# Gated linear attention and a squared-ReLU MLP on one core: an instruction order worked out again with other durations and rank shifts

## The chip, the core and the metric

The kernel runs on one core of one Trainium2 chip. The metric is the device time of one execution in microseconds (us). Three executions of the kernel before took 702.45, 704.4 and 1441.48 us; the median is 704.4 us. A profile was taken of one execution.

## The reference, cut to what matters

```python
# q, k, v, a_re, a_im: (4, 8, 768, 48), fp32
mag = sqrt(a_re**2 + a_im**2)
a = (a_re + 1j * a_im) * minimum(mag, 0.999) / (mag + 1e-6)
for t in range(768):                       # per batch and head, state S is 48 x 48, complex
    S = a[t][:, None] * S + outer(k[t], v[t])
    y[t] = q[t] @ S.real
x = y.transpose(0, 2, 1, 3).reshape(3072, 384)
h = x @ w_in                               # 384 x 2048
out = maximum(h, 0)**2 @ w_out             # 2048 x 384
```

## The kernel before

The 3072 rows are cut into six tiles of 512 time steps (`NU = 6`, index `n` below). For each tile there are three stages.

* **chain(n)**, mostly VectorE (DVE) and ScalarE (ACT). The gates are loaded in natural layout, normalised (`roots`, `normalise`, lines 956 to 999), multiplied up over groups of four steps (`inner`, lines 1011 to 1019), transposed on TensorE (PE) in `totals` (line 1065), scanned on DVE (`scan`, `product`, lines 1157 to 1224) and transposed back (`back`). Then `inverse`, `factors` and `twist` make the inverse products (1033 to 1045, 1114 to 1129), and `apply` multiplies q and k by the running products (1285 to 1299). `gather` moves k to another layout by DMA (line 1340).
* **pairs(n)**, for four pairs of heads. `turn_pe` (tiles 0 and 1, PE transposes of line 1401, ACT copies of line 1405) or `turn` (later tiles: DVE transposes of line 1378 and DMAs) lays q and k out by feature. `score` multiplies them (PE line 1419) and masks the result (DVE line 1422); `keep` makes the state sums (PE line 1447, DVE lines 1456 and 1458); `mix` makes y (PE lines 1471 and 1475, ACT copy of line 1481), and SyncE (SP) DMAs bring y into `xT`.
* **dense(n, grp)**, two groups of 256 rows: `part_of` is x times w_in (PE line 1511), `relu` the activation (ACT lines 1542 and 1543). The second product is plain for tile 0 (PE line 1557) and otherwise `seven` or `eight`, a scheme with fewer products (PE line 1619, DVE lines 1634 and 1643).

The weights arrive as 64-bit numbers and are made into fp32 on the chip: `fetch` loads a piece (GpSimd queue, POOL, line 817), `convert` makes it fp32 (ACT lines 830 and 834, DVE lines 836, 840 and 843). Eight pieces are w_in and eight are w_out. `inspect` reads them once more near the end, and `verdict` decides whether the fast result holds.

No engine chooses its order at run time. Every stage only hands **steps** to a planner (`Plan.add`): an engine, a duration, what it reads and writes, and a rank. `Plan.order` plays these steps through once while the kernel is being built. At each moment it takes, among the steps of an engine whose inputs are ready by its own clock, the one of the lowest rank. The start times that it arrives at give the order in which the instructions are emitted, and so the fixed order of every engine's queue and of every DMA queue. The durations are thus never a limit on the chip: they only decide the order.

Ranks are pairs such as `(PAIR, n)`, and 100 times the first plus the second is compared: pairs of tile n have 100 + n, its chain 200 + n, dense work 300 + n, the conversion of w_in 200.3 and that of w_out 200.6. `Plan.shift` adds to these numbers by hand, for a group of steps (`groups`) or for one step (`single`), numbered in the order in which they were added.

Two further things hang on the planner. Where PE is planned to stand idle and one of the banks d0 to d2 is free, `order` puts **idle products** there (a product of the identity with itself, emitted from line 735), which write nothing that is used; their number is the planned idle time, less 0.3 us, over `EACH`. And a PE step that follows a planned stop of over 2.5 us is planned as slower for a while (`STOP`, `COLD`):

```python
if spare and stop > self.FILL:
    self.fill[n] = int((stop - 0.3) / self.EACH), spare[0]
elif stop > self.STOP:
    warm = t + self.COLD
```

Of the kernel before, what the change touches and what calls it, by code (L numbers as in the profile page):

```python
# [480 lines left out]
class Plan:  # L481
# [7 lines left out]
    FILL, EACH = 0.8, 0.22  # L489
# [8 lines left out]
    def add(self, eng, dur, reads, writes, fn, rank, wire=None, group=None, after=(), slack=False):  # L498

        n = len(self.steps)  # L500
# [4 lines left out]
        for k in reads:  # L505
            deps.update(self.wrote.get(k, (None, ()))[1])
        for k in writes:
# [12 lines left out]
        self.steps.append((eng, dur, sorted(deps), fn, rank, wire, slack))  # L520
# [10 lines left out]
    def order(self):  # L531
# [11 lines left out]
        bus, warm = 0.0, 6.0  # L543
# [18 lines left out]
        for _ in steps:  # L562
# [10 lines left out]
            _, dur, _, _, _, wire, _ = steps[n]  # L573
# [48 lines left out]
def fast_path(ctx, tc, q, k, v, a_re, a_im, moe_w_in, moe_w_out, out, flag):  # L622
# [6 lines left out]
    C = 128  # L629
# [129 lines left out]
    def dma(q, reads, writes, fn, rank, size, lat=1.8, group=None):  # L759
        name, dur = ("POOL", 0.55) if q is pool else ("SP" if q is sp else "ACT", 0.6)  # L760
        step(name, dur, reads, writes, fn, rank, (lat, size), group)
# [52 lines left out]
    def fetch(i, early=True):  # L814
# [3 lines left out]
            (CONV, i), 2 * PW * 4 * C, 4.0)  # L818

    def convert(i):  # L820
# [11 lines left out]
        if mixed:  # L832

            step("ACT", 1.92, keys + [("lo", i)], [("lo", i, 1)], lambda: act.activation(
                out=part(F16, 1), in_=part(I16, 3), func=AF.Copy, scale=2.0 ** -60), rank)
        step("DVE", ts2(PW), keys, wk, lambda: dve.tensor_scalar(
# [9 lines left out]
    def inspect(i):  # L846
# [6 lines left out]
        if i == 0:  # L853
# [5 lines left out]
            rank, 2 * PW * 4 * C)  # L859
# [61 lines left out]
    def chain(n):  # L921
# [81 lines left out]
        def inner(z):  # L1003
# [16 lines left out]
            for c in range(1, W):  # L1020
                step("DVE", 2 * tt(m) + 0.06, [("a", z)], key(z, 0), lambda c=c: terms(c), ahead)
                step("DVE", 2 * tt(m // 2) + 0.06, key(z, 0), [("a", z)],
                     lambda c=c: joined(c), ahead)
            xh = xn.rearrange("p r (h d) -> p r h d", h=H)[:, :, ts(z, HH)]
            step("ACT", ac(Z // W), [("a", z)], [("xn", 0, z), ("xn", 1, z)],
# [33 lines left out]
        def turned(src, put, by, keys, rk):  # L1059
# [6 lines left out]
            step("PE", 0.12 * NM, keys, [(b,)], go, rk)  # L1066
# [8 lines left out]
        def totals(j):  # L1075
# [4 lines left out]
            step("ACT", ac(DM), [b], [("e", j)], lambda: act.copy(  # L1080
                out=e[:, j], in_=p4), ahead)
            if j == 1:
                step("ACT", ac(DM), [b], [("e", 2)], lambda: act.mul(
                    out=e[:, 2], in_=p4, mul=-1.0), ahead)
            if not ends:
                step("ACT", ac(NM), [b], [("el", j)], lambda: act.copy(
                    out=el[:, j], in_=last), ahead)
                if j == 1:
                    step("ACT", ac(NM), [b], [("el", 2)], lambda: act.mul(
# [13 lines left out]
        def factors(rk):  # L1103
# [15 lines left out]
            step("DVE", 2 * tt(DM) + ts2(DM), E, E + [("x",)], scaled, rk)  # L1119
# [11 lines left out]
            step("DVE", 3 * tt(DM), E + [("x",)], E + X, refined, rk)  # L1131
# [13 lines left out]
        def product(dst, xx, y, reads, writes, at=KC[0], own=None, rk=ahead):  # L1145
# [16 lines left out]
            step("DVE", 3 * tt(cnt) + 0.24, reads, writes + (own or K), go, rk)  # L1162
# [11 lines left out]
        def scan():  # L1174
# [8 lines left out]
            step("DVE", 0.5, E, I, sums_of, ahead)  # L1183
# [7 lines left out]
            step("DVE", 0.33, I, I, tops, ahead)  # L1191
# [3 lines left out]
            for s in (1, 2, 4):  # L1195
                if s < span:
                    product(tv[:, 0:2, :, s:span], tv[:, 0:2, :, s:span],
                            lambda lo, hi, s=s: tv[:, lo:hi, :, 0:span - s], I, I)
                    step("DVE", 0.18, I, I, lambda s=s: minus(top, s, span, tv), ahead)
# [5 lines left out]
            step("DVE", 0.16, I, I, shift, ahead)  # L1205
# [8 lines left out]
            step("DVE", 0.36, I, I, finish_inc, ahead)  # L1214
            for r in range(2):
                def last(r=r):
                    own = [f[:, r].rearrange("p (w x g) -> p w x g", w=4, x=4) for f in gg]
                    for o, y, ro in ((own[0], 0, r), (own[1], 2 - r, 1 - r)):
# [8 lines left out]
                step("DVE", 3 * tt(384) + 0.28, E + I, K + [("xn", r, 0), ("xn", r, 1)], last,  # L1227
                     ahead)
# [14 lines left out]
        def back(j):  # L1243
            ps, b = turned(lambda m: xn[:, j, ts(m, C)], natural, ident,
                           [("xn", j, 0), ("xn", j, 1)], ahead)
            step("ACT", ac(DM), [b], [("xn", j, 0), ("xn", j, 1)], lambda: act.copy(  # L1246
# [82 lines left out]
    def gather(n, z, p, np):  # L1329
# [5 lines left out]
        for i in needs(n):  # L1335
            for c in range(W):
# [5 lines left out]
                    rank, 32 * w * 4, group=(n, p))  # L1342
# [13 lines left out]
    def pairs(n, which):  # L1356
# [31 lines left out]
        def turn_pe(i):  # L1388
# [5 lines left out]
            for c in range(W):  # L1394
# [7 lines left out]
                step("PE", 0.46, [("f", z, 2 * (i % 2) + j) for j in range(2)], [(b,)],  # L1402
# [417 lines left out]
```

## Time and profile before

| | |
|---|---|
| times of three executions | 702.45, 704.4, 1441.48 us |
| span of the profiled execution | 703.0 us |
| PE, DVE, ACT, POOL busy | 686.7, 572.7, 350.4, 174.7 us |
| idle products on PE | 530 instructions, 62.5 us |
| mean granted PE clock | 0.993 |

The profiled execution's own time is its span of 703.0 us; nothing beside the span is given for it, and it lies between the lowest time and the median. "Busy" is the time in which an engine has an instruction in work. An fp32 product of 128 rows is two instructions in the trace, a transpose one. Windows are counted in us from the start of the span. In a row of the timeline the number in brackets is the time that the engine stood idle just before, with what ended it.

### The profile page before, as it was taken

To read this page: it belongs to the slowest core of one execution; us is meant where nothing else is said; L and a number is where in the kernel's file an instruction comes from. 1 tells how busy PE (TensorE), PEld (TensorE's weight loads), DVE (VectorE), ACT (ScalarE), POOL (GpSimd) and SP (SyncE) were. 2 spreads that over 40 slices of the span, in tenths; PEclk is the share of its full clock that TensorE was granted. 3 is DMA by queue.
4 is the path that set the end of the run, shared out by engine and by line. 5 is a ranking of instruction groups with operands and counts; after the bars stand their busy time and mean duration, and the time that the engine had idled before them with its cause. 6 is when DMAs were issued, how large, how long until landed. Compare 5 with 4: busy or idle time off the path is not lost.

```text
span 703.0 us, 12562 instructions
## 1 busy us (share of the span) xinstructions
PE 686.7 (98%) x4572; PEld 623.3 (89%) x4572; DVE 572.7 (81%) x1177; ACT 350.4 (50%) x582; POOL 174.7 (25%) x334
## 2 busy tenths in 40 slices
PE   9998999999999999999999999999999999999996
PEld 9998888667778999998998898999989989989995
DVE  6989989999889689997898598998689998337721
ACT  7575379955575534376424557333657242132230
POOL 6502543052300003205044050033230033032100
PEclk9999989999999999999999999999999999999998
DMA  9740459130530004735037570037550035288600
GB/s 283 216 176 19 116 133 310 56 68 23 158 114 23 1 19 122 190 91 145 6 97 194 124 154 12 1 95 184 136 150 1 24 90 139 59 289 279 202 7 22
DMA packets 56679, 79.58 MB, mean 113 GB/s; under 512 B 11008, under 2 KB 38784, under 8 KB 56608
## 3 DMA queue, kind: packets, MB, share of 16 engines
q0 software_dynamic: 15232, 40.72, 19.2%
q1 hardware_dynamic: 37088, 32.89, 18.2%
q10 hardware_dynamic: 4288, 5.08, 2.7%
q8 instruction: 38, 0.62, 0.4%
q14 instruction: 33, 0.27, 0.1%
HBM read 48.76 MB, written 4.72 MB: 76 GB/s over the span
## 4 chain that ended last, share of the span: by engine, by line
PE 67%; DVE 20%; ACT 3%; issue 3%; DMA 3%; POOL 2%; SPq 1%; DVEq 0%; ACTq 0%; POOLq 0%
PE d L1511 26%; PE d L1619 22%; PE sc L1419 5%; PE tr L1447 3%; PE yp L1471 3%; PE d L1557 2%; DVE f L1299 2%; DVE f L1285 2%; PE yp L1475 2%; DVE f L1011 2%; PE tr L1511 2%; POOL T L917 1%; PE sc L1511 1%; DVE aq L1289 1%; DVE w L840 1%
## 5 line engine op out<-in xcount | busy, mean ns | idle before, releaser
L1511 PE MATMUL d<-xT,w 128*128 128x256 f32 x1056 | 235.5, 380 | 0.7 <-DVE ot L1643 0.7
L1511 PEld LDWEIGHTS d<-xT,w 128*128 128x128 f32 x1056 | 198.8, 190 | 28.7 <-DVE ot L1643 1.5
L1619 PE MATMUL d<-w,g 128*128 128x192 f32 x768 | 132.8, 327 | 0.0
L1619 PEld LDWEIGHTS d<-w,g 128*128 128x128 f32 x768 | 124.9, 190 | 1.6 <-issue 0.9
L1542 ACT ACTIVATE g<-d 128x512 f32<-128x512 f32 x88 | 52.3, 594 | 127.9 <-PE d L1511 94.3
L1340 POOL DMA_DIRECT2D KC<-f x160 | 78.5, 498 | 110.9 <-issue 47.4
L1580 POOL DMA_DIRECT2D out_dram<-ot x22 | 12.6, 572 | 241.8 <-DVE ot L1643 146.4
L1619 PE MATMUL d<-T,g 128*128 128x192 f32 x384 | 66.5, 327 | 0.3 <-DVE g L1634 0.3
L735 PE MATMUL d<-ident 128*128 128x128 f32 x530 | 62.5, 282 | 1.5 <-POOL ident masks.py:199 1.5
L1619 PEld LDWEIGHTS d<-T,g 128*128 128x128 f32 x384 | 62.8, 190 | 0.8 <-DVE g L1634 0.6
L735 PEld LDWEIGHTS d<-ident 128*128 128x128 f32 x530 | 61.9, 198 | 1.5 <-POOL ident masks.py:199 1.5
L917 POOL DMA_DIRECT2D v<-in_v_dram x80 | 46.4, 587 | 65.5 <-PE yp L1471 30.5
L1543 ACT ACTIVATE g<-g 128x512 f32<-128x512 f32 x96 | 60.6, 631 | 3.1
L1634 DVE TENSOR_TENSOR g<-g 128x512 f32<-128x512 f32 x64 | 43.0, 683 | 22.2 <-ACT g L1543 15.7
L1419 PE MATMUL sc<-QT 96*128 96x128 f32 x368 | 48.0, 285 | 0.8 <-ACT QT L1405 0.8
L1481 ACT COPY yt<-yp 112x512 f32<-112x512 f32 x24 | 26.2, 1091 | 44.5 <-PE yp L1475 44.5
L1419 PEld LDWEIGHTS sc<-QT 96*128 96x128 f32 x368 | 45.0, 198 | 2.7 <-issue 1.3
L1285 DVE TENSOR_TENSOR f<-aq,xn 128x384 f32<-128x384 f32 (+1 forms) x64 | 45.1, 748 | 2.3 <-ACT xn L1246 2.3
L1299 DVE TENSOR_TENSOR f<-aq 128x384 f32<-128x384 f32 (+1 forms) x64 | 45.0, 751 | 0.6
L1557 PE MATMUL d<-w,g 128*128 128x384 f32 x128 | 44.2, 488 | 0.2 <-DVE w L843 0.2
L1422 DVE TENSOR_TENSOR A<-sc,mask 128x512 f32<-128x512 f32 x45 | 29.9, 681 | 14.6 <-PE sc L1419 14.6
L1011 DVE TENSOR_TENSOR f<-aq 128x384 f32<-128x384 f32 x72 | 36.8, 552 | 0.8
(195 smaller groups left out, 989.5 us busy)
## 6 DMA issues: line engine op xcount, KB each, us to landing
QT<-aq SPq DMA_DIRECT2D x128, 64.0 KB, 2.2
f<-in_moe_w_in_dram POOLq DMA_DIRECT2D x8, 768.0 KB, 7.2
f<-in_moe_w_out_dram POOLq DMA_DIRECT2D x8, 768.0 KB, 6.3
KC<-f POOLq DMA_DIRECT2D x104, 48.0 KB, 2.4
out_dram<-ot POOLq DMA_DIRECT2D x22, 192.0 KB, 2.3
QT<-aq ACTq DMA_DIRECT2D x64, 64.0 KB, 2.4
v<-in_v_dram POOLq DMA_DIRECT2D x80, 48.0 KB, 3.3
xT<-yt SPq DMA_DIRECT2D x36, 96.0 KB, 2.5
```

The costliest lines, as they stand in the source:

```text
L735: plan = Plan(lambda b: pe.matmul(bank[b][:, 0:C], lhsT=ident, rhs=ident, start=True, stop=True), ["d2", "d1", "d0"], lambda ap: tc.nc.val ...
L917: lambda i=i, c=c, src=src: pool.dma_start(out=t[32 * c:32 * c + 32, i], in_=src[c]), vrank, 32 * 1536, 4.0,
L1011: dve.tensor_tensor(out=f, in0=a[:, :, :, c - 1], in1=a[:, j, :, c].unsqueeze(1).to_broadcast([C, 2, HH, D]), op=ALU.mult)
L1285: lambda j=j, r=r: dve.tensor_tensor(out=f4[:, j, r], in0=a[:, r], in1=over(j), op=ALU.mult), late[z])
L1299: lambda j=j, r=r, o=o: dve.tensor_tensor(out=o[:, :, :, r * D:(r + 1) * D], in0=qk[:, j], in1=a[:, r], op=ALU.mult), late[z])
L1340: lambda i=i, c=c, queue=queue: queue.dma_start(out=kc[32 * c:32 * c + 32, i], in_=nat[32 * i:32 * i + 32, c]),
L1419: pe.matmul(sa[:, j], lhsT=T[:, j, 1, h], rhs=T[:, j, 0, h], start=True, stop=True)
L1511: pe.matmul(ps, lhsT=w1[:, f // FP, m, ts(f % FP, C)], rhs=xT[:, n % 2, m, ts(grp, G)], start=(m == 0), stop=(m == NM - 1))
L1542: act.activation(out=o, in_=ps, func=AF.Relu)
L1543: act.activation(out=o, in_=o, func=AF.Square)
L1557: pe.matmul(ps, lhsT=gt[:, f % 2, ts(i, C)], rhs=w2[:, f], start=(f == 0), stop=(f == NF - 1))
L1619: pe.matmul(bank[b][:, 0:DH], lhsT=g4[:, r, j], rhs=w(j), start=first and j == 0, stop=last and j == NT - 1)
```

## The change

All steps, their inputs and outputs and what each instruction computes stay as they are. What changes is what the planner is told, and so the order and the number of idle products.

* **Idle products.** Each is put at 0.224 in place of 0.22 us, and in front of the very first PE step the time that is taken off the planned idle time is 3.3 in place of 0.3 us (`BEGIN`).
* **Dependent DVE steps.** A DVE step that reads what the DVE step just before it wrote is planned 0.11 us longer (`TIGHT`), unless it is marked with `slack`; the steps of the scan are marked.
* **PE modes.** A PE step is planned 0.1 us longer when `mix` follows something else, or something else follows `mix` (`SWITCH`).
* **DMA issues.** 0.57 us on POOL, 0.62 on SP and 0.53 on ACT, in place of 0.55, 0.6 and 0.6; 0.74 for a piece of the weights, and 0.5 for `gather` on POOL.
* **Other durations**, most of them by under 0.2 us; the larger ones are `mix` (2.0 to 1.68), its ACT copy (1.11 to 0.85), one conversion on ACT (1.92 to 1.68) and the collection of the checks (2.6 to 3.4).
* **Rank shifts.** The 13 groups and 9 single steps of before are replaced by 18 groups and 15 single steps.

By the planner's numbering the shifts of after fall on these steps. Tile 0: the loads of three pieces of w_in, of one of w_out, and of one part of v change places on POOL's queue (groups 6, 9, 11; singles 13, 157); the first squares on ACT (17), the scaling of the gates (30), `inner` (32), the carry (49), and `keep` on PE, which goes from rank 100 to 197.31 (76). The conversion of w_out on ACT is put back by 0.73 (92), one DVE conversion of w_out to 300 (single 396), one of w_in forward (single 47). Tile 1: `inner` goes ahead of everything on DVE (120), and `score` goes from 101 to 201.32 (161); one product of `eight` is put forward (single 865). Tile 2: `inverse` is put forward (207), `mix` and its DMAs back (232, 234). Of tiles 3 to 5 only `score` of tile 3 (296, by 0.03) and one step of `inner` of tile 4 (single 1763, 98.01 before) still have a shift; the shifts of before on tiles 3 to 5 (258, 297, 352, 354, 372, 394, 1425, 1687, 1759) are gone.

```diff
-    FILL, EACH = 0.8, 0.22
+    FILL, EACH, BEGIN = 0.8, 0.224, 3.3
+    TIGHT, SWITCH = 0.11, 0.1
...
     def add(...):
...
             deps.update(self.wrote.get(k, (None, ()))[1])
+        raw = frozenset(deps)
...
-        self.steps.append((eng, dur, sorted(deps), fn, rank, wire, slack))
+        self.steps.append((eng, dur, sorted(deps), fn, rank, wire, slack, mode, raw))
...
                 if spare and stop > self.FILL:
-                    self.fill[n] = int((stop - 0.3) / self.EACH), spare[0]
+                    lost = 0.3 if free[e] else self.BEGIN
+                    self.fill[n] = max(0, int((stop - lost) / self.EACH)), spare[0]
                 elif stop > self.STOP:
                     warm = t + self.COLD
                 if t < warm:
                     dur += min(dur, 0.5 * (warm - t))
+                if steps[n][7] != mode:
+                    mode = steps[n][7]
+                    dur += self.SWITCH
+            if e == "DVE":
+                if last in steps[n][8] and not steps[n][6]:
+                    dur += self.TIGHT
+                last = n
...
-        name, dur = ("POOL", 0.55) if q is pool else ("SP" if q is sp else "ACT", 0.6)
-        step(name, dur, reads, writes, fn, rank, (lat, size), group)
+        name, took = ("POOL", 0.57) if q is pool else ("SP", 0.62) if q is sp else ("ACT", 0.53)
+        step(name, dur or took, reads, writes, fn, rank, (lat, size), group)
...
-            step("PE", 2.0, [("A", got["A", i, h]) for h in range(2)]
+            step("PE", 1.68, [("A", got["A", i, h]) for h in range(2)]
                  + [("v", vs(n)), ("QT", got["T", i]), ("St", s), ("S", n % 2, i)],
-                 [("yp",)], go, rank)
+                 [("yp",)], go, rank, mode=1)
...
     plan.shift(
-        groups={77: 100.01, 80: 2.93, 100: -0.9, 159: -2.64, 161: 0.18, 232: 0.28, 234: 103.28,
-            258: 1.25, 297: 0.64, 352: 0.34, 354: 0.6, 372: 0.17, 394: -2.31},
-        single={368: 0.46, 613: -197.29, 866: 8.98, 921: 0.46, 1273: -97.94, 1425: -0.29,
-            1687: -97.83, 1759: 1.33, 1763: 98.01})
+        groups={6: 1.28, 9: -1.2, 11: -1.48, 17: -1103.06, 30: -1.64, 32: 0.05, 49: 98.13, 76:
+            97.31, 77: 0.34, 92: 0.73, 118: 0.1, 120: -1109.71, 149: 0.92, 161: 100.32, 207:
+            -4.84, 232: 2.72, 234: 11.3, 296: 0.03},
+        single={8: 3.77, 13: -396.32, 47: -202.85, 63: 0.13, 91: 0.01, 117: 0.25, 157: -2.3, 200:
+            0.02, 396: 99.37, 438: -0.68, 453: 1.12, 613: -1.81, 705: 2.59, 865: -100.86, 1763:
+            100.21})
```

More of the change, by code (lines that the diff above doesn't have):

```diff
@@ L1182, in sums_of @@
                 minus(inc)
-            step("DVE", 0.5, E, I, sums_of, ahead)
+            step("DVE", 0.42, E, I, sums_of, ahead, slack=True)
             for w in range(1, 4):
@@ L1190, in tops @@
                 minus(top)
-            step("DVE", 0.33, I, I, tops, ahead)
+            step("DVE", 0.31, I, I, tops, ahead, slack=True)
             span = 4 if cross else 8
@@ L1213, in finish_inc @@
                 minus(incx)
-            step("DVE", 0.36, I, I, finish_inc, ahead)
+            step("DVE", 0.34, I, I, finish_inc, ahead, slack=True)
             for r in range(2):
```

68 lines of the change are left out of this document (35 added, 33 removed).

## The prediction

> **What bounds the kernel now.** I read the page first, then the busy time by stage, then the idle products by stage, then the timeline of the first 215 us.
>
> ```profile
> span 703.0 us, 12562 instructions
> PE 686.7 (98%) x4572; PEld 623.3 (89%) x4572; DVE 572.7 (81%) x1177; ACT 350.4 (50%) x582; POOL 174.7 (25%) x334
> ...
> PEclk9999989999999999999999999999999999999998
> ```
>
> PE is busy for 686.7 of 703.0 us, but that says little alone, since idle products count as busy. The stages are shown first for all engines (length; busy us and instructions of PE, PE's weight loads, DVE, ACT and POOL; granted clock; DMA share; GB/s) and then for line 735 alone, the idle products, with two groups of the page (instructions, busy us, mean ns, idle us before).
>
> ```profile
> 0.00:38.30 38.30, 36.78 (x308) 36.78 (x309) 31.15 (x52) 23.45 (x38) 21.15 (x49) 1.00 0.82 256
> 38.30:64.00 25.70, 25.70 (x232) 25.63 (x231) 23.08 (x73) 20.19 (x31) 0.00 (x0) 1.00 0.21 80
> 64.00:85.00 21.00, 17.52 (x182) 15.33 (x179) 20.41 (x46) 8.44 (x14) 11.84 (x25) 1.00 0.36 86
> 85.00:92.00 7.00, 7.00 (x35) 6.87 (x36) 5.56 (x12) 1.16 (x2) 3.85 (x8) 0.52 0.46 116
> 92.00:100.00 8.00, 8.00 (x100) 7.30 (x98) 6.77 (x12) 6.37 (x9) 0.93 (x2) 1.00 0.57 144
> 100.00:180.00 80.00, 77.73 (x344) 58.91 (x343) 77.03 (x166) 59.97 (x99) 29.01 (x51) 1.00 0.43 117
> 180.00:680.00 500.00, 497.99 (x3286) 456.77 (x3285) 402.66 (x809) 230.51 (x389) 107.95 (x201) 1.00 0.39 108
> ```
>
> ```profile
> 0.00:38.30 38.30, 36.78 (x308) 36.78 (x308) 1.00 0.82 256
> 38.30:64.00 25.70, 24.79 (x218) 24.37 (x217) 1.00 0.21 80
> ```
>
> ```profile
> L735 PE MATMUL d<-ident 128*128 128x128 f32 x530 | 62.5, 282 | 1.5 <-POOL ident masks.py:199 1.5
> L1557 PE MATMUL d<-w,g 128*128 128x384 f32 x128 | 44.2, 488 | 0.2 <-DVE w L843 0.2
> ```
>
> There are three regimes. Up to 64 us PE has next to nothing to do: 36.78 + 24.79 = 61.6 of its 62.5 busy us are idle products, and DVE sets the pace with tile 0's chain (54.2 of 64.0 us). From 64 to 180 us DVE and PE are both nearly full: DVE 20.41 of 21 and 77.03 of 80, PE 77.73 of 80. From 180 to 680 us PE is the bound: it stands idle for 2.0 of 500 us. What follows the last products is one addition and a store, and the change does not touch them:
>
> ```profile
> 693.20 2.76 PE L1619 MATMUL d<-T,g 128*128 128x192 f32 x16
> 696.39 0.38 ACTq L1575 DMA_DIRECT2D out_dram<-ot  x1
> ```
>
> PE's useful products are the same before and after. An order can only give back what PE loses, and nearly all of that lies ahead of 180 us: the wait for tile 0, 3.5 us of idle time at 64 to 85, a half clock at 85 to 92, 2.3 us of idle time at 100 to 180. Behind that there are 2.0 us to win. This caps a gain; it does not cap a loss.
>
> **Part 1: the first idle products (`BEGIN`, `EACH`).**
>
> ```profile
> 34.69 0.51 ACT L1026 COPY xn<-aq 128x384 f32<-128x384 f32 x1 [5.32 <-DVE aq L1019]
> 38.34 0.82 PE L1065 MATMUL tr<-perm,xn 128*128 128x128 f32 x6
> 39.39 0.95 DVE L840 SCALAR_TENSOR_TENSOR w<-w,w 128x768 uint32<-128x768 uint32 x1 [1.82 <-issue]
> 63.86 0.38 PE L1401 MATMUL d<-ident,f 128*96 128x128 f32 x2
> 65.31 1.74 PE L1401 MATMUL d<-ident,f 128*96 128x128 f32 x14 [1.07 <-DVE f L1299]
> ```
>
> The scan of tile 0 needs both copies of line 1026. The second ends at 34.69 + 0.51 = 35.20 us, but PE comes to its transposes at 38.34: it is still working off 308 instructions, that is 154 idle products. They are 3.1 us too many. With the old numbers 154 products stand for (154 x 0.22) + 0.3 = 34.2 us of planned idle time. The new numbers make (34.2 - 3.3) / 0.224 = 137 of that, 17 fewer, or 17 x 0.224 = 3.8 us, so PE would be waiting at 35.2 us. What this is worth is what DVE lost: it stood idle for 1.82 us ahead of 39.39 and used the rest of the delay for other steps that it had to do anyway. Gain 1.8 us; bounds 1.8 and 3.1. The last run of idle products ends at 63.86, and PE then waits once more, 1.07 us for DVE, so a shorter run there is worth nothing: that wait would only begin earlier.
>
> **Part 2: `keep` of tile 0 later (group 76).** These are the rows around the half clock.
>
> ```profile
> 82.85 0.51 PE L1447 MATMUL tr<-v,KC 128*96 128x48 f32 x4 [0.64 <-DMA KC<-f]
> 83.78 1.00 PE L1447 MATMUL tr<-v,KC 128*96 128x48 f32 x8 [0.42 <-DMA KC<-f]
> 84.99 0.85 PE L1447 MATMUL tr<-v,KC 128*96 128x48 f32 x4 [0.21 <-DMA KC<-f]
> 85.64 3.75 PE L1419 MATMUL sc<-QT 96*128 96x128 f32 x16
> 89.18 3.17 PE L1401 MATMUL d<-ident,f 128*96 128x128 f32 x16
> 93.96 2.05 PE L1419 MATMUL sc<-QT 96*128 96x128 f32 x16
> ```
>
> PE waits 0.64 + 0.42 + 0.21 = 1.27 us for `gather`'s DMAs at the head of `keep`, and the scores of line 1419, which need no such DMA, stand behind it. Right after that the clock is granted at 0.52 for 7 us: 16 score instructions take 3.75 in place of 2.05 us, and 16 transposes 3.17 in place of some 2.0 us (14 took 1.74 at 65.31). That is 1.7 + 1.2 = 2.9 us, in all 4.2 us between 82 and 92. Moving `keep` from rank 100 to 197.31 lets scores go first, so that the waits can be covered. Whether the half clock goes too is open: the planner lowers its clock only after a stop of 2.5 us, and here no single wait in the stage was over 1.07 us. Bounds: a gain of 4.2 us, and a loss of 2.9 us if a second such stretch comes, since `keep` no longer fills the holes ahead. I take half of the gain, 2.1 us, as the waits are what the new rank surely moves.
>
> The Trainium skill, TensorE: Matmul & The Clock Gate, Part 1 on the clock gate, has the array fall to half rate after an idle window of about 3.4 us. No run here shows such a window ahead of 85 us, and the clock fell all the same; by that rule the half clock would be an accident, not coming back, and the sum below would be 2.1 us lower.
>
> **Part 3: dependent DVE steps (`TIGHT`).**
>
> ```profile
> 56.89 0.55 DVE L1114 TENSOR_TENSOR e<-e 128x384 f32<-128x384 f32 x1
> 57.47 0.36 DVE L1115 TENSOR_SCALAR x<-e 128x384 f32<-128x384 f32 x1
> 59.39 1.02 DVE L1289 TENSOR_TENSOR aq<-f 128x384 f32<-128x384 f32 x2
> ```
>
> Line 1115 reads what 1114 wrote and starts 57.47 - 56.89 = 0.58 us after it; two independent instructions of the same size take 1.02 us together, so the second starts 1.02 - 0.55 = 0.47 us after the first. A dependent follower costs 0.11 us more, just the new constant. The planner can now put an independent step between two dependent ones. Most of DVE's work ahead of 64 us cannot be parted so: the scan is one step after another. I count on some ten places, 1.0 us (bounds 0 and 3).
>
> The Trainium skill, VectorE: DVE Perf Modes, the section on the DRAIN that cannot be avoided, says that the next operation does not start until the pipe is empty and that chaining without a semaphore saves nothing. By that alone this part would be worth 0 and the sum 1.0 us higher; the two spacings above, 0.58 and 0.47 us, speak for the constant.
>
> **Part 4: the stage from 100 to 215 us (groups 92, 118, 120, 149, 161; singles 47, 63, 396, 705).**
>
> ```profile
> 99.67 2.86 PE L1511 MATMUL d<-xT,w 128*128 128x256 f32 x12
> 105.73 1.13 PE L1511 MATMUL tr<-xT,w 128*128 128x256 f32 x4 [1.32 <-DVE w L843]
> 127.77 4.14 PE L1557 MATMUL d<-w,g 128*128 128x384 f32 x12 [0.20 <-DVE w L843]
> 156.28 0.55 PE L1065 MATMUL tr<-ident,xn 128*128 128x128 f32 x3 [0.47 <-DVE xn L1224]
> 212.60 1.56 PE L1557 MATMUL d<-w,g 128*128 128x384 f32 x4
> ```
>
> PE's waits here are for DVE: 1.32 us for w_in, 0.20 for w_out, 0.47 for tile 1's scan. DVE does two things at once, conversions and chain(1), and is full (77.03 of 80 us). The dense products of tile 0 (lines 1511 and 1557, the last at 212.60) are what PE does while it waits for tile 1. If the front ends some 5 us sooner, PE wants everything 5 us sooner, but DVE has only 80 - 77.03 = 3.0 us of idle time in which to follow. I give back 1.0 us for this, and set against it half of PE's 2.3 us of idle time, which the shifts are aimed at: 1.1 us. Bounds: +5 us (the front's gain given back) and -2.3.
>
> **Part 5: the rest.** The new DMA issue times agree with the old order's rows, and POOL and SP are no bound, so I put them at nothing; the moved loads of w_in, w_out and v land while PE does idle products, and cost something only if a piece comes late for its conversion.
>
> ```profile
> L1340 POOL DMA_DIRECT2D KC<-f x160 | 78.5, 498 | 110.9 <-issue 47.4
> L858 POOL DMA_DIRECT2D f<-in_moe_w_in_dram x8 | 6.0, 750 | 10.2 <-DVE odd L865 9.9 <-issue 0.3
> L1481 ACT COPY yt<-yp 112x512 f32<-112x512 f32 x24 | 26.2, 1091 | 44.5 <-PE yp L1475 44.5
> ```
>
> 0.498 and 0.750 us stand beside the new 0.5 and 0.74. The copy of line 1481 does not fit: 1.091 us against the new 0.85, though the next step on ACT can start before the record ends. The shifts on tiles 3 to 5 fall away; there PE idles 2.0 us in 500 now, so the most that can be gained is 2.0 and a loss is open. Each of these three tiles has one such stage, and I allow 2 us for each, as for the 2.3 us at 100 to 180: +6. I take 0.
>
> **The sum.** 703.0 - 1.8 - 2.1 - 1.0 + 1.0 - 1.1 = 698.0 us, 5.0 us or 0.7% faster. The span of 703.0 is within the runs shown (702.45 to 704.4, the median), so 698.0 is 0.9% under the median. What can about be told from no change in this kernel is 2%, 14 us: under 690.3 or over 718.5 us.
>
> **Rivals.**
>
> *The whole front comes in.* 3.1 + 4.2 + 3.0 + 2.3 + 2.0 = 14.6 us, every upper bound at once: 688.4 us. For it: the losses are real and the new constants are those of the trace. Against it: DVE has only 3.0 us of idle time at 100 to 180 with which to follow.
>
> *The gain is given back, or the order hardly differs.* Parts 1 to 3 win 4.9 us, and PE waits 5 us longer for DVE between 100 and 215, as DVE's work is the same: 703 us. For it: DVE is full there. Against it: PE idles there for just 2.3 us, so DVE was not late by much.
>
> *Slower: PE runs dry ahead of tile 1.* The place is 120 to 215 us. `inner` of tile 1 goes ahead of everything on DVE, conversion of w_out goes back on ACT and for one piece on DVE, and the scores of tile 1 go behind the chain. Each product of line 1557 needs its piece of w_out. Tile 0 has 128 such instructions with 44.2 us of PE work; if not quite half of it has to wait for its pieces while the other filler (line 1511) is used up, PE stands for 20 us, and 703.0 - 1.8 + 20 = 721.2. It decides from 718.5 - 701.2 = 17.3 us of standing, 50 of the 128 instructions. A PE that stands may also be granted half its clock, as after 1.27 us of waits above. For it: both engines are full and one must give. Against it: planned durations come closer to the rows, so such a hole would show in the plan.
>
> **How the numbers follow.** The forecast has 0.36, with a range of its own of 692 to 701. The whole front 0.20, the gain given back 0.16, PE dry 0.28. Faster by over 2% is the whole front, 0.20; slower by over 2% is PE dry, 0.28; within 2% are the other two, 0.52. The range is 686 to 722: it takes in 688.4 and 721.2 and leaves out the tails of these two, some 0.2 together. The predicted time is the forecast's, 698.0.
>
> **What would show it.** Part 1 is right if some 274 instructions of line 735 stand ahead of the first line 1065, that starts at about 35 us, and DVE's 1.82 us are gone. Part 2 is right if PE waits for line 1340's DMAs less and the clock at 80 to 100 us is 1.00; wrong if there is a half clock of 7 us or more. Part 3: the last transposes of line 1065 in tile 0 come sooner by more than part 1 explains. Part 4: PE's idle time at 100 to 215 stays under 3 us; over 10 us, with waits of line 1557 for line 843, it is the slower rival. The forecast fails if PE's idle time behind 180 us grows by several us, or if the dense products of tile 0 start no sooner than now, at 99.67 us.

## The result, and the profile after

The kernel after takes 695.7 us (median of four runs, 694.43 to 697.89), the kernel before beside it 703.75 us (702.45, 703.1, 704.4 and 1441.48). The ratio, which leaves out the run of 1441.48 us, is 0.9897 with a 95% interval of 0.9871 to 0.9923: 1.0% faster, or 8 us by the medians. That is real, but within the 2% that the prediction called about no change. The profiled execution of after took 696.35 us with a span of 694.6 us; spans are compared with spans below: 703.0 to 694.6, a gain of 8.4 us.

First the page of after, beginning with the busy time of each engine, then the group of idle products.

```profile
span 694.6 us, 12508 instructions
PE 678.3 (98%) x4546; PEld 617.6 (89%) x4546; DVE 572.1 (82%) x1177; ACT 348.8 (50%) x582; POOL 175.6 (25%) x334
...
PEclk9999999999999999999999999999999999999998
...
L746 PE MATMUL d<-ident 128*128 128x128 f32 x504 | 58.6, 279 | 1.5 <-POOL ident masks.py:199 1.5
```

PE is busy for 8.4 us less, of which 62.5 - 58.6 = 3.9 us are idle products. DVE has the same work. (Lines of after stand 11 or 12 further down than in before: 1065 is 1076, 1511 is 1523, 1557 is 1569, 843 is 854, 735 is 746. An edit that adds lines moves them further: in e1 by 1 against before, in e4 by 4 against after.) Now the stages, in the same windows as in the prediction:

```profile
0.00:38.30 38.30, 36.11 (x307) 35.88 (x308) 30.19 (x54) 27.04 (x48) 20.68 (x48) 1.00 0.83 267
38.30:64.00 25.70, 23.73 (x211) 23.36 (x209) 24.33 (x73) 16.75 (x22) 2.44 (x6) 1.00 0.20 68
64.00:85.00 21.00, 20.14 (x212) 18.98 (x210) 20.76 (x46) 9.90 (x18) 14.34 (x29) 1.00 0.45 112
85.00:92.00 7.00, 6.33 (x77) 5.88 (x78) 6.83 (x17) 4.63 (x7) 0.04 (x1) 1.00 0.30 76
92.00:100.00 8.00, 4.54 (x32) 3.50 (x29) 7.84 (x10) 6.21 (x8) 7.42 (x13) 0.81 1.07 223
100.00:180.00 80.00, 79.14 (x376) 60.71 (x375) 74.69 (x167) 55.38 (x96) 24.85 (x45) 1.00 0.45 119
180.00:680.00 500.00, 499.97 (x3295) 461.26 (x3294) 405.77 (x811) 228.93 (x389) 105.83 (x197) 1.00 0.39 106
```

Three things differ. PE is idle for 0.86 us at 64 to 85 in place of 3.48, and has twice the instructions at 85 to 92 at full clock. At 92 to 100 there is a new hole of 3.46 us with a lower clock behind it. And behind 180 us PE's idle time is 0.03 us in place of 2.01.

The timeline of PE shows where the 8.4 us arise: the end of the first idle products, the new hole, the first dense product of tile 1 and the last product.

```profile
1.52 33.73 PE L746 MATMUL d<-ident 128*128 128x128 f32 x286 [1.52 <-POOL ident masks.py:199]
35.09 0.27 PE L1076 MATMUL tr<-perm,xn 128*128 128x128 f32 x1
...
93.21 0.70 PE L1523 MATMUL d<-xT,w 128*128 128x256 f32 x2
97.36 3.88 PE L1523 MATMUL d<-xT,w 128*128 128x256 f32 x10 [3.46 <-DMA xT<-yt]
...
209.64 2.86 PE L1523 MATMUL d<-xT,w 128*128 128x256 f32 x12
...
685.56 2.76 PE L1631 MATMUL d<-T,g 128*128 128x192 f32 x16
```

In before tile 1's first dense product begins at the first row below, and the last product ends at 693.20 + 2.76 = 695.96 (a row of the prediction).

```profile
213.99 1.89 PE L1511 MATMUL d<-xT,w 128*128 128x256 f32 x8
```

So the gain is cut in three:

| stretch | before | after | gain |
|---|---|---|---|
| front: start to tile 1's first dense product | 213.99 | 209.64 | 4.35 |
| tail: from there to the end of the last product | 481.97 | 478.68 | 3.29 |
| end: from there to the end of the span | 7.04 | 6.28 | 0.76 |

The end varies between 5.2 and 7.1 us over the kernels below, with the same instructions; it is left aside.

### The profile page after: what moved, and what is told of

Its sections match the earlier page's. It is cut to its first block, busy times and chain, and to the rows that moved or that the text cites. A ratio compares the mean times of both kernels' runs of the same rounds, so it can differ in the third digit from the quotient of the medians.

```text
span 694.6 us, 12508 instructions
## 1 busy us (share of the span) xinstructions
PE 678.3 (98%) x4546; PEld 617.6 (89%) x4546; DVE 572.1 (82%) x1177; ACT 348.8 (50%) x582; POOL 175.6 (25%) x334
## 4 chain that ended last, share of the span: by engine, by line
PE 77%; DVE 18%; DMA 2%; ACT 1%; issue 1%; SPq 0%; ACTq 0%; DVEq 0%
PE d L1523 30%; PE d L1631 27%; PE sc L1431 5%; PE tr L1459 3%; PE yp L1483 3%; PE d L1569 3%; PE yp L1487 2%; DVE f L1022 2%; DVE f L1310 1%; DVE w L854 1%; DVE f L1296 1%; DMA aq<-in_a_im_dram 1%; PE tr L1413 1%; PE sc L1523 1%; PE tr L1523 1%
## 5 line engine op out<-in xcount | busy, mean ns | idle before, releaser
L746 PE MATMUL d<-ident 128*128 128x128 f32 x504 | 58.6, 279 | 1.5 <-POOL ident masks.py:199 1.5
L746 PEld LDWEIGHTS d<-ident 128*128 128x128 f32 x504 | 58.1, 196 | 1.5 <-POOL ident masks.py:199 1.5
L1655 DVE TENSOR_TENSOR ot<-ot,d 128x192 f32<-128x192 f32 x64 | 21.7, 350 | 20.3 <-PE d L1631 19.9
```

The lines of the kernel that those rows point to most:

```text
L746: plan = Plan(lambda b: pe.matmul(bank[b][:, 0:C], lhsT=ident, rhs=ident, start=True, stop=True), ["d2", "d1", "d0"], lambda ap: tc.nc.val ...
```

## The experiments

"Before" in these comparisons took 704.0 to 704.3 us. Step numbers are the planner's.

### Idle products alone, and everything but them

```diff
e1_fill_on_before, against before
-    FILL, EACH = 0.8, 0.22
+    FILL, EACH, BEGIN = 0.8, 0.224, 3.3
...
-                    self.fill[n] = int((stop - 0.3) / self.EACH), spare[0]
+                    lost = 0.3 if free[e] else self.BEGIN
+                    self.fill[n] = max(0, int((stop - lost) / self.EACH)), spare[0]

e2_old_fill_on_after, against after
-    FILL, EACH, BEGIN = 0.8, 0.224, 3.3
+    FILL, EACH, BEGIN = 0.8, 0.22, 0.3
```

> The kernel before, every instruction in its old order; only the number of idle products is worked out with the new numbers (0.224 and 3.3), which takes 16 of them from in front of the first transposes of line 1065 and two more behind. Theory of part 1: PE comes to the transposes at about 35 us in place of 38.3, DVE's idle time of 1.82 us ahead of the scan goes, and the run is 1.8 us shorter (ratio 0.9974). Rival: what the front wins is lost again at the wait for the second half of tile 0's products (line 1401, 65 us) or in the half clock, ratio 1.000.

> The kernel after, every instruction in its new order; only the number of idle products is worked out with the old numbers (0.22 and 0.3), which puts 16 more in front of the first transposes. If the fill is worth what part 1 says, this is 1.8 to 3.6 us slower than the kernel after (ratio to before 0.992 to 0.995 in place of 0.990). If DVE does other work meanwhile and the front is not set by the transposes, it is the same as after, 0.990.

The order of before with the new numbers took 702.16 us, ratio 0.9977 (0.9963 to 0.9991), 1.9 us shorter where 1.8 were expected. The order of after with the old numbers took 700.92 us, ratio 0.9953 (0.9941 to 0.9966): some 4 us longer than after by the ratios, 5 by the medians, where 1.8 to 3.6 were expected. From PE's timeline of the first, then of the second kernel: the first transposes, tile 0's first scores, tile 1's first dense product, the last product. Behind them stand the first scores of before and of after.

```profile
34.26 0.27 PE L1066 MATMUL tr<-perm,xn 128*128 128x128 f32 x1
...
65.94 2.05 PE L1420 MATMUL sc<-QT 96*128 96x128 f32 x16 [0.81 <-ACT QT L1406]
...
210.24 1.89 PE L1512 MATMUL d<-xT,w 128*128 128x256 f32 x8
...
691.69 2.76 PE L1620 MATMUL d<-T,g 128*128 128x192 f32 x16
```

```profile
39.44 0.82 PE L1076 MATMUL tr<-perm,xn 128*128 128x128 f32 x6
...
68.83 2.05 PE L1431 MATMUL sc<-QT 96*128 96x128 f32 x16 [0.81 <-ACT QT L1417]
...
214.31 1.99 PE L1523 MATMUL d<-xT,w 128*128 128x256 f32 x8
...
689.98 2.76 PE L1631 MATMUL d<-T,g 128*128 128x192 f32 x16
```

```profile
67.86 2.05 PE L1419 MATMUL sc<-QT 96*128 96x128 f32 x16 [0.81 <-ACT QT L1405]
```

```profile
66.96 2.05 PE L1431 MATMUL sc<-QT 96*128 96x128 f32 x16 [0.82 <-ACT QT L1417]
```

With the start of tile 0's first dense product (99.67, 95.85, 96.32 and 93.21 us) this cuts the front in three:

| stretch | before | e1 | e2 | after |
|---|---|---|---|---|
| start to tile 0's first scores | 67.86 | 65.94 | 68.83 | 66.96 |
| pairs: from there to tile 0's first dense product | 31.81 | 29.91 | 27.49 | 26.25 |
| from there to tile 1's first dense product | 114.32 | 114.39 | 117.99 | 116.43 |
| tail | 481.97 | 484.21 | 478.43 | 478.68 |

Up to the first scores the idle products are worth 1.92 us on the old order and 1.87 us on the new one, although the first transposes come 4.08 and 4.35 us sooner: for the rest of the delay DVE had other work. What e1 wins beyond that, another 1.90 us, stands in the pairs, where the half clock is shorter in its profiled execution (granted clock 0.59 at 84 to 88 us, 1.00 from 88). In e2 the delay of 1.87 us grows to 4.67 us at tile 1: its wait for `xT` is 4.21 us in place of 3.46, and the clock is 0.50 from 96 to 104 us, in after 0.62 from 96 to 100 us.

The new order loses 1.0 us up to the first scores, wins 3.7 to 4.3 us in the pairs, and loses 2.0 to 3.7 us again up to tile 1. So the front with the old numbers (214.31 us) is as long as that of before (213.99) because gains and losses cancel.

On the old order the front wins 213.99 - 210.24 = 3.75 us, but the tail then takes 694.45 - 210.24 = 484.21 us, 2.2 more than before; 1.5 us are left at the last product, and 1.9 in the medians. The new order's tail takes 692.74 - 214.31 = 478.43 us even with the old numbers, as in after. The tail of the first kernel has one long wait that before has not, the first row of its waits of PE behind 180 us (us in total, times, longest):

```profile
PE d L1620 <- DVE g L1635: 2.4, 1, 2.4
```

### The half clock

```diff
e3_scores_before_keep, in the emission of before
+        block = [n for n in order if n in (344, 345, 346, 347)]
+        order = [n for n in order if n not in block]
+        i = order.index(342) + 1
+        order = order[:i] + block + order[i:]
```

> The kernel before with one move in the finished order: the keep of tile 0's third pair (two PE steps and the two DVE additions behind them) comes after that pair's scores. Theory of part 2: the waits of 0.64, 0.42 and 0.21 us for the gather's DMAs at 82 to 85 us are covered by the scores, the half clock behind them does not come, and the first dense product starts 3 to 4 us sooner than at 99.7; the run is 2 to 4 us shorter, ratio 0.994 to 0.997. Rival: DVE sets the pace up to 180 us, the first dense product starts sooner but tile 1's pairs do not, ratio 0.999 to 1.000.

It took 703.54 us, ratio 0.9991 (0.9982 to 1.0): the expected rival, not the theory. Its stages, from a profiled execution of 705.69 us, 2.2 above the median:

```profile
85.00:92.00 7.00, 5.96 (x66) 5.16 (x65) 5.76 (x12) 4.12 (x7) 3.54 (x8) 1.00 0.46 118
92.00:100.00 8.00, 6.29 (x66) 5.50 (x65) 7.86 (x14) 4.51 (x6) 3.31 (x6) 1.00 0.64 158
...
180.00:680.00 500.00, 496.26 (x3271) 455.00 (x3269) 400.53 (x805) 230.05 (x389) 106.72 (x199) 1.00 0.39 107
```

The half clock is gone (1.00 in place of 0.52), and the first dense product comes at 97.3 in place of 99.67 us. At tile 1 1.2 us of that are left, and behind 180 us PE stands idle for 3.74 us, 1.7 more than before; how much of this belongs to that one execution is not known. In the end the move was worth 0.5 us, and at most 1.3 by the interval.

That the half clock itself is worth no more does not follow. Of the 64 runs of before that stand beside e1 to e12, 13 have a mean clock of 0.997 or more, and in each of the three sets these are shorter on average than the others, by 1.6, 1.8 and 2.3 us. The mean does not say where in a run the clock was low, so this is a hint only; it would fit a move that costs elsewhere what the clock gives.

### The new hole at 93 us

In after the first dense product waits 3.46 us for `xT`, which SP brings. SP's queue shows why: four loads of gates are issued ahead of the five transfers to `xT`.

```profile
89.81 1.34 SPq L914 DMA_DIRECT2D aq<-in_a_re_dram  x2
91.26 1.25 SPq L914 DMA_DIRECT2D aq<-in_a_im_dram  x2
92.61 3.10 SPq L1501 DMA_DIRECT2D xT<-yt  x5
```

```diff
e4_xT_ahead_of_loads, in the emission of after
+        block = [n for n in order if n in (509, 510, 511, 512)]
+        order = [n for n in order if n not in block]
+        i = order.index(352) + 1
+        order = order[:i] + block + order[i:]
```

> The kernel after with one move in the finished order: on SP's queue the four loads of tile 1's second half of the gates come after the three stores of y into xT of tile 0's third pair, not before them. Theory: PE's wait of 3.46 us for xT at 94 us is made by the queue, so it falls by the time of the four issues, some 2.4 us, the lower clock at 92 to 100 us goes with it, and the run is 2.4 to 4 us shorter than after (ratio to before 0.984 to 0.987). Rival: the loads come 2 us later, tile 1's normalisation with them, DVE's wait of 2.5 us for ACT at 104 us grows by that, and the run stays at 0.990.

It took 695.96 us, ratio 0.9889 (0.9875 to 0.9904), as after. PE's wait for `xT` is gone. In its place stand 1.08 and 1.0 us of waits for converted weights and 1.7 us for which the profile names no cause, and the lower clock comes later (waits of PE between 64 and 180 us, then two windows; the short row has length, PE busy, clock, DMA share, GB/s):

```profile
PE d L1527 <- issue: 1.7, 1, 1.7
PE sc L1527 <- DVE w L858: 1.1, 1, 1.1
PE d L1573 <- DVE w L858: 1.0, 1, 1.0
...
100.00:104.00 4.00, 3.28 (x9) 0.57 1.13 207
...
100.00:180.00 80.00, 77.89 (x363) 59.51 (x364) 76.47 (x169) 58.44 (x100) 25.45 (x46) 0.98 0.46 122
```

The first wait for weights is one that after hides behind the hole: this conversion ends at 97.84 us here and at 97.98 in after. So 2.8 us of other waits and the lower clock take the place of 3.46 us, PE is 0.54 us ahead behind them (105.72 against 106.26), and the last wait, 1.0 us in place of 0.5, takes that. The move also costs time on DVE, as the rival in the expectation had it. The loads of tile 1's gates now come later, and DVE stands for them by way of ACT, where in after it has no wait (97.90 us):

```profile
100.93 0.96 DVE L979 TENSOR_TENSOR f<-f 128x768 f32<-128x768 f32 x1 [3.09 <-ACT f L956]
```

Tile 1's first dense product comes at 209.62 us, in after at 209.64: what PE does sooner it waits for later.

### The squares in the order in which the gates land

After has a wait on DVE that before has not (before waits once for this tensor, in the first half): the square of the imaginary part stands at the head of the queue until its load lands, with other work behind it.

```profile
9.48 0.96 DVE L972 TENSOR_TENSOR f<-aq 128x768 f32<-128x768 f32 x1 [2.27 <-DMA aq<-in_a_im_dram]
```

The edit puts the two squares of this half (steps 84 and 85) further back, and shortens the first run of idle products to match.

```diff
e5_squares_in_landing_order, in the emission of after
+        block = [n for n in order if n in (84,)]
+        order = [n for n in order if n not in block]
+        i = order.index(75) + 1
+        order = order[:i] + block + order[i:]
+        block = [n for n in order if n in (85,)]
+        order = [n for n in order if n not in block]
+        i = order.index(83) + 1
+        order = order[:i] + block + order[i:]
+        self.fill[120] = 134, self.fill[120][1]

e6_squares_and_xT: this and the edit before it
```

> The kernel after with two DVE steps of the first 12 us moved in the finished order, and 9 idle products fewer ahead of the first transposes. The trace of after shows DVE standing 2.27 us for the last load of the gates (a_im of the second half) at 9.48 us, with products behind it that are ready at 7.6 us; the load of a_re had landed earlier. Here the two squares of the second half stand in the order in which their loads land, with the ready products between and ahead, as before. Theory: DVE's front comes 1.5 to 2.0 us sooner, with the idle products cut by 9 x 0.224 = 2.0 us PE follows, and the run is 1.5 to 2 us shorter than after (ratio to before 0.986 to 0.988). Rival: the time is lost again to the SP queue and the store of xT at 94 us, ratio 0.990.

> The move of the squares and the cut of idle products, together with the move of xT's stores ahead of tile 1's loads on SP. If the front and the queue are two separate losses, this is 2 to 3 us shorter than after (ratio to before 0.985 to 0.987); if one hides the other, it is like the move of the squares alone.

The first took 694.55 us, ratio 0.9854 (0.9829 to 0.988), the second 695.03 us, 0.9872 (0.9848 to 0.9897); expected were 1.5 to 2 and 2 to 3 us less than after, the medians are 1.2 and 0.7 us less. Up to the first dense product the first is 1.7 us ahead of after (91.55 against 93.21); at tile 1 0.5 us are left (209.16). Its profiled execution, at 696.08 us, is the longest of its five, and the five times fall as the mean clock rises, from 696.08 us at 0.993 to 691.98 us at 0.998. It is the fastest version here, but its interval overlaps with that of after, so that it is faster than after is not shown.

### Durations and shifts taken apart

Six kernels: the durations of before or after (each with its own numbers for idle products), and the shifts of before, of after or none. In the last two the durations are those of after with `TIGHT` at 0.

```diff
e7_new_durations_old_shifts: after, with the plan.shift(...) of before
e8_old_durations_new_shifts: before, with the plan.shift(...) of after
e9_new_durations_no_shifts: after, with
+    plan.shift(groups={}, single={})
e10_old_durations_no_shifts: before, with the same empty line
e11_no_shifts_no_dependent_cost: as e9, and
-    TIGHT, SWITCH = 0.11, 0.1
+    TIGHT, SWITCH = 0.0, 0.1
e12_no_dependent_cost: after, with only this last edit
```

> The kernel after with the rank shifts of before: only the durations, the added costs and the idle products are new. Theory A, better durations make a better order by themselves: ratio 0.985 to 0.995. Theory B, the shifts only fit the durations with which they were found, so a mixture loses what the old shifts had won: slower than before, ratio 1.005 to 1.02.

> The kernel before with the rank shifts of after: old durations, old idle products. Theory A: the new shifts carry the gain, ratio 0.990 to 0.996 (short of the idle products). Theory B, shifts fit only their durations: slower than before, ratio 1.003 to 1.015.

> The changed kernel with an empty shift table: corrected durations and new idle-product numbers alone. Theory A (the later stages gain through the durations, the front through the idle products and shifts that fit): from tile 1's first dense product to the last product it takes 478 to 480 us, as in the changed kernel (478.7) and in the run with the old shifts (479.3); what the missing shifts cost stands ahead of 215 us, 0 to 6 us, so 696 to 703 us. Theory B (the tail is set by the shifts or by chance in each order): its tail lies anywhere from 478 to 486 us.

> The kernel before with an empty shift table. Theory A: the stretch from tile 1's first dense product to the last product takes 482 to 485 us, as in all four runs so far that have the old durations (482.0 to 484.3), and the whole is 4 us or more slower than the run with new durations and no shifts: 703 to 712 us. Theory B: its tail is no longer than that of the new durations without shifts, and the two differ by less than 2 us there.

> New durations and no shifts, but the 0.11 us for a dependent VectorE operation taken out. If that constant carries the gain of the later stages, the stretch behind tile 1's first dense product goes back to 482 to 485 us. If it is the other durations (and the constant only reorders tile 0's chain, as the prediction's Part 3 had it), the stretch stays at 478 to 480 us and the front moves by 3 us at most.

> The changed kernel with its shifts, the 0.11 us for a dependent VectorE operation taken out. The prediction's Part 3 has that constant at 1.0 us (bounds 0 and 3): 696.5 to 699. Rival: the shifts were fitted to durations that hold the constant, so without it they do harm, as the old shifts did under the new durations (708): 700 to 708 us, the loss ahead of 215 us.

Median us, and the ratio to before with its interval:

| durations | no shifts | shifts of before | shifts of after |
|---|---|---|---|
| of before | 705.64; 1.0022 (1.0004 to 1.0041) | 704.0 to 704.3 | 705.3; 1.0016 (1.0001 to 1.0031) |
| of after | 710.82; 1.0109 (1.0073 to 1.0145) | 708.2; 1.0064 (1.0039 to 1.0089) | 695.7; 0.9897 (0.9871 to 0.9923) |
| of after, `TIGHT` 0 | 703.03; 0.9988 (0.9969 to 1.0007) | not tried | 703.44; 0.9988 (0.9974 to 1.0002) |

This is the main finding. Only one field of the table is clearly faster than before. Without shifts the corrected durations make the kernel 5 us *slower* than the old ones (710.82 against 705.64), although they were put closer to the trace (0.5 and 0.74 us stand beside rows of 0.498 and 0.750; the 0.85 us of `mix`'s copy, beside 1.091, do not fit). The shifts of after are worth 15 us on the durations for which they were made, and nothing on the others; those of before are worth 1.5 us on theirs. The same holds for `TIGHT`: taking it out costs 7.7 us with the shifts of after, and wins 7.8 us without shifts. Neither the durations nor the shifts carry the gain; their fit does. Whether closer durations allow a better fit, or the table of after was just the luckier find, these runs do not tell: they hold only one table made for each set of durations.

The profiled executions by stretch, as above. Those of e8 (707.97 us) and e12 (704.13 us) lie 2.7 and 0.7 us above their medians, and in e12 some dense products of tile 0 come ahead of its last `mix`:

| stretch | e7 | e8 | e9 | e10 | e11 | e12 |
|---|---|---|---|---|---|---|
| start to tile 0's first scores | 63.04 | 70.72 | 63.86 | 67.11 | 65.83 | 70.20 |
| pairs of tile 0 | 40.29 | 27.42 | 39.96 | 32.62 | 33.65 | 24.63 |
| from there to tile 1's first dense product | 117.76 | 118.52 | 115.51 | 116.49 | 111.82 | 119.24 |
| tail | 479.26 | 484.07 | 484.67 | 481.89 | 484.07 | 482.22 |

Where the time goes in the slow ones can be read. In e7 and e9 it is the pairs of tile 0, with 40 us in place of 26.25 in after. Their last `mix` ends at 103.4 and 103.9 us in place of 93.3: between `keep` and `mix` PE has only idle products. In e7 (PE timeline):

```profile
99.14 0.51 PE L1459 MATMUL tr<-v,KC 128*96 128x48 f32 x4 [0.78 <-DMA KC<-f]
99.48 2.24 PE L746 MATMUL d<-ident 128*128 128x128 f32 x18
101.65 0.65 PE L1483 MATMUL yp<-A,v 128*48 128x128 f32 x8
```

In e9 the dense products of tile 0 are used up at 206.2 us, and PE has nothing but idle products between the pieces of tile 1's pairs:

```profile
203.44 2.75 PE L1569 MATMUL d<-w,g 128*128 128x384 f32 x8
...
207.09 0.68 PE L746 MATMUL d<-ident 128*128 128x128 f32 x4
...
210.14 1.28 PE L746 MATMUL d<-ident 128*128 128x128 f32 x10
```

With two more rows of this kind it is 4.1 us of idle products at 200 to 220 us, where none of the kernels with shifts has any (e10 has 3.45 us there and e11 0.90). It is half of the mechanism of the prediction's slower rival, in small: the other work is used up, but no product of line 1569 waits for w_out.

The theories on the tail did not hold as they were written. With shifts and the full new durations the tail takes 478.4 to 479.3 us (after, e2, e4 to e7). With shifts and old durations it takes 482.0 to 484.2 (before, e1, e3, e8), and e12 takes 696.29 - 214.07 = 482.2. So far theory A of e9 and e10 is right, and the dependent operations are needed for it. But without shifts it fails: 484.67 us in e9, 481.89 in e10, 484.07 in e11. There the boundary holds other work (some of tile 1's `mix` comes behind the first dense product), so PE's idle time is the better measure. From 180 to 680 us, in after with `TIGHT` 0 (e12) and in e9:

```profile
180.00:680.00 500.00, 497.72 (x3287) 456.54 (x3284) 401.46 (x806) 229.45 (x390) 105.31 (x196) 1.00 0.39 108
```

```profile
180.00:680.00 500.00, 497.41 (x3324) 457.65 (x3324) 407.17 (x818) 228.61 (x385) 109.82 (x204) 1.00 0.40 109
```

That is 2.28 and 2.59 us; e10 has 1.53 and e11 2.26. e9 has the full new durations and stands idle all the same. But it waits for something else, in the one view of PE's waits behind 180 us: two waits for `xT`, none for a DVE result. In e12, with `TIGHT` out, PE waits for DVE (`ot`) and for k's DMA:

```profile
PE d L1523 <- DMA xT<-yt: 2.3, 2, 1.5
```

```profile
PE d L1523 <- DVE ot L1655: 1.0, 1, 1.0
PE tr L1459 <- DMA KC<-f: 0.7, 1, 0.7
```

Behind 180 us PE waits for DVE results for at most 0.5 us in the seven kernels with the full new durations, for 0.6 and 1.2 us in the two with `TIGHT` 0, and for 1.0 to 4.0 us in the four with the old durations and either table of shifts. e10, with old durations and no shifts, has no such wait. So it fits all kernels but one, and is not shown, that the new durations bring DVE's results in time behind tile 1; the waits of e9 and e10 for SP and ACT show that this alone is not enough.

## Why the prediction was right or wrong

The forecast of 698.0 us is 2.3 us above the median, and its kind (some us faster, within 2%) is what came. Its sum starts from a span, though, and a time is some 1.7 us longer than its span (696.35 and 694.6): span against span the forecast is 3.4 us too long, 5.0 us of gain in place of 8.4. The sum of its front terms, -5.0, stands beside 4.35 measured at tile 1's first dense product, but this is in part luck. By the stretches of the first experiment, Parts 1 and 3 were to win 2.8 us and 0.90 came up to the first scores; Part 2 was to win 2.1 and the pairs won 5.56; Part 4 was to win 0.1 and 2.11 were lost up to tile 1. The errors cancel.

**Part 1, idle products: right in mechanism and size at its place.** 286 instructions stand ahead of the first transposes (some 274 expected), these start at 35.09 us (35 expected), and DVE no longer stands for 1.82 us. "What this is worth is what DVE lost", 1.8 us, is what e1 and e2 show at the first scores, 1.92 and 1.87 us. (The 1.9 us at the end of e1 come about by way of 3.75 us won at tile 1 and 2.2 lost in the tail, so that agreement is luck.) What the sum left out is that a delay at 67 us meets other waits later: on the new order it has grown to 214.31 - 209.64 = 4.7 us at tile 1, above the upper bound of 3.1.

**Part 2, `keep` later: right, too small.** The waits for `KC` in tile 0 and the half clock at 85 to 92 us are gone, and the pairs are 5.56 us shorter, more than the bound of 4.2, which left out the 0.33 us of a wait for `f` and the 0.90 us of idle products that before has in this stretch. Taking half was not wrong in kind: behind the pairs 2.11 us are given back, partly in the wait for `xT`. Against it stands e3, which removes the waits for `KC` and the half clock in the old order and gains at most 1.3 us at the end. The test "clock at 80 to 100 us is 1.00" failed, with 0.81 at 92 to 100. What that lower clock costs is not shown: in e4 it is not gone but comes at 100 to 104 us.

By the Trainium skill, TensorE: Matmul & The Clock Gate, Part 1, the lower clock behind the wait of 3.46 us is what an idle window of about 3.4 us brings, and the trace agrees (granted clock 0.62 at 96 to 100 us). The half clock of before, with 1.27 us of waits ahead of it, stays outside that rule, and it came again in other kernels (below), so it was no accident.

**Part 3, `TIGHT`: wrong in kind.** It was costed as 1.0 us won by parting dependent steps in tile 0. With the same numbers for idle products the last transposes of tile 0 end 0.7 us later in the new order than in the old (52.76 in after, 52.05 in e1), and the first scores come 1.0 us later; a gain would have had to show there. The constant's effect is 7.7 us one way or 7.8 the other, depending on the shifts: it steers which order comes out, and is no saving to be added up. These runs say nothing of the 0.11 us itself.

**Part 4, 100 to 215 us: right in kind, too small.** PE's idle time at 100 to 180 fell from 2.27 to 0.86 us; half of it was expected. Of the 6.46 us by which the first dense product came sooner, 4.35 are left at tile 1, so 2.1 us were given back where 1.0 had been taken. The reason given, that DVE is full, is not shown: gains of 2.3 and 1.7 us at the first dense product shrink to 1.2 and 0.5 at tile 1 in e3 and e5, but e1 keeps 3.75 of 3.82 with DVE as busy (77.10 us at 100 to 180). In after the wait for `xT` stands in this stretch, made by SP's queue, which Part 5 called no bound; e4 shows other waits of nearly the same length behind it.

**Part 5, the rest: wrong.** It was put at nothing, with a gain of 2.0 at most. The tail gained 3.29 us. These are its windows, of before and of after (length, PE busy, clock, DMA share, GB/s):

```profile
213.99:695.96 481.97, 480.29 (x3107) 1.00 0.38 104
```

```profile
209.64:688.32 478.68, 478.65 (x3108) 1.00 0.38 105
```

1.65 us are idle time, nearly all that there was, and 1.64 us are busy time, with the same number of instructions to within one: they lie closer together. Against the fear that the tiles without their shifts would lose 2 us each, there is no loss. The argument "at most 2.0" failed because busy time was read as time without loss. Why the products lie closer stays open.

**The rivals.** The slower one did not come: line 1569 waits for 0.5 us in all for w_out between 30 and 180 us, and PE does not run dry. e9 shows a part of its mechanism, with 4.1 us of idle products ahead of tile 1, but far from the 17 us that it needed. That the gain is given back is what happens to e3, and in part to e1. The argument for the forecast that "planned durations come closer to the rows, so such a hole would show in the plan" was weak: e9 has those durations and the hole.

## What to carry to other kernels

A planner that always takes the ready step of the lowest rank is not made better by corrected durations alone: here they lost 5 us without ranks fitted to them and won 8 us with them, so durations and ranks are to be changed and measured together. A gain inside one stage is not the gain of the kernel: of 2.3 us (`keep` later in the old order) 1.2 were left at the next tile, of 1.7 (the squares) 0.5, and of the 3.46 us for `xT` nothing, as other waits stood behind it; but what e1 gained was kept up to there. Idle work put in front of the first useful instruction must end before its input is there; an overshoot of 4 us cost 1.9 us at the next stage here, because another engine had work to do meanwhile, and more than that later on. And one profile is one execution: where a step of a proof rests on a row, look where the time of that execution lies among the others.

## What the runs showed of the hardware that was not expected

The clock of PE falls to half after short waits too. In e11 only two waits for `KC`, of 0.70 and 0.49 us with products between them, stand ahead of it (PE timeline, then 92 to 96 us: length, PE busy, clock, DMA share, GB/s):

```profile
89.53 1.02 PE L1459 MATMUL tr<-v,KC 128*96 128x48 f32 x8 [0.70 <-DMA KC<-f]
91.03 0.51 PE L1459 MATMUL tr<-v,KC 128*96 128x48 f32 x4 [0.49 <-DMA KC<-f]
91.38 3.20 PE L1431 MATMUL sc<-QT 96*128 96x128 f32 x16
...
92.00:96.00 4.00, 4.00 (x22) 0.50 0.65 154
```

As in before it is the stage of `keep` in tile 0. There the 16 score instructions took 3.75 us, here 3.20, at full clock 2.05. In e1 they took 3.07 us, behind waits of 0.38 and 0.41 us, and in e4 the clock was 0.57 at 100 to 104 us, behind waits of 1.08 and 1.70 us. But it stayed at 1.00 after the three waits of 0.2 to 0.8 us in e9, and in e3 after waits of 1.04, 0.86 and 1.71 us. So neither the longest wait nor their sum tells when it falls; the cause remains open.
